# Attention, a gated MLP and a spatial-gating MLP on one core: small pooling and splitting work dealt out anew between VectorE, GpSimd and ScalarE, with a new order of the whole program

## The chip, the cores and the metric

The kernel runs on one core of one Trainium2 chip. The metric is the device time of one execution, in microseconds (us); smaller is better. The core has TensorE (PE: matmuls, and PEld its weight loads), VectorE (DVE), ScalarE (ACT), GpSimd (POOL) and SyncE (SP, which here issues all the transfers between DRAM and the on-chip memory). Each engine works through its own instructions in the order of its program and waits where a semaphore says that an operand, or a buffer, isn't ready.

## The reference

Eight batches of 576 positions, three parts that feed each other, all in float32:

```python
# 1. attention, 8 heads of 64, keys and values averaged over groups of 8 positions (72 of them)
k_p = k.reshape(B, H, 72, 8, D).mean(axis=3);  v_p = ... the same
attn = softmax(scale * q @ k_p^T);  x = attn @ v_p          # x: (8, 576, 512)
# 2. MLP with a convolution of width 3 along the positions as its gate
h = relu(x @ w_in)                                          # 512 -> 1024
x = (h * sigmoid(conv3(h))) @ w_out                         # 1024 -> 512
# 3. MLP with a spatial gate
h = gelu_tanh(x @ w_in2);  u, v = h[..., :512], h[..., 512:]
v_n = (v - mean(v)) / sqrt(var(v) + 1e-6) * g_ln            # over the 512 features
v_s = einsum('ts,bsd->btd', w_sg, v_n) + b_sg               # over the 576 positions
out = x + (u * v_s) @ w_out2                                # 512 -> 512
```

## The kernel before

Every float32 factor of a product is split into a high part, rounded to the matmul's input type, and a low part, the rest. A product is then three matmuls (high x high, low x high, high x low) summed in PSUM. So each operand costs a cast (mostly ACT) and a subtraction (`subtract`, L133, the instruction on L134; by DVE unless another engine is given).

The work goes in three stages that run into each other. Stage A (0 to about 540 us) is attention and the first MLP, batch after batch. `t_k` loads the keys of a batch in three blocks (`i` 0, 1, 2) and pools them with `pool_sum`: DVE does it in one reduction (L249), POOL as a tree of three additions (L251, L253, L255). For batch 0, DVE takes blocks 0 and 2 and POOL block 1. `t_kfin` transposes the pooled keys on PE (L292) and copies them to `KBT` with ACT (L295, L296) and DVE (L298, L301). The scores (L419), exponentials, their split (`eTh`, `eTl`), the attention product (L106 into `psa`), and the two matmuls of the MLP follow; their weights are loaded and split by `weight` along the way. Stage B (about 540 to 735 us) is the first matmul of the second MLP by a seven-product scheme. `t_v2` makes the v half of a block of rows: gelu on ACT, mean and variance on DVE (L804, L805), reciprocal deviation `rstd` on POOL (L808, L809), normalisation on DVE (L812), store to DRAM (`vs`, L816). It runs 18 times. Stage C (about 731 us to the end) loads the normalised v back (`vf`), forms sums on POOL (L948), splits them (`sc`: cast on ACT L617, subtraction L134), multiplies with the split `w_sg` (L767), lets DVE evict each quadrant with bias and gain (L997, into `tmp`) and POOL multiply it with u (L1001), splits the result (`g`) and does the last matmul (L99 to L101), to which DVE adds the residual (L1053). The 64 positions that don't fill a tile of 128 go through `t_vr` (`vr`: cast L956, subtraction of 64x512). `t_w_out2` loads and splits the four blocks of the last weight (`w4`, `w6`, `T3`, `T4`).

What sets the order is one long string, `ORDER`. Each part of the program (`t_k`, `t_v2`, ...) is a generator; a token such as `k1.0` or `n2.5` runs it to its next `yield`, and each engine's instructions are chained in the order in which the tokens issue them. Nothing reorders them later: an instruction that waits holds up whatever stands behind it on its engine. SP's transfers are chained likewise.

Of the kernel before, what the change touches and what calls it, by code (L numbers as in the profile page):

```python
# [11 lines left out]
AF = mybir.ActivationFunctionType  # L12
ALU = mybir.AluOpType
# [13 lines left out]
def pooled_attention_gated_mlps(  # L27
# [218 lines left out]
    def pool_sum(eng, raw, dst, n):  # L246
        a = raw[0:n]
        if eng is nc.vector:
            eng.tensor_reduce(out=dst, in_=a.rearrange("p a (r d) -> p a d r", r=POOL), axis=AX.X, op=ALU.add)  # L249
            return  # L250
        eng.tensor_tensor(out=a[:, :, 0:256], in0=a[:, :, 0:256], in1=a[:, :, 256:512], op=ALU.add)  # L251
        yield
        eng.tensor_tensor(out=a[:, :, 0:128], in0=a[:, :, 0:128], in1=a[:, :, 128:256], op=ALU.add)  # L253
        yield
        eng.tensor_tensor(out=dst, in0=a[:, :, 0:64], in1=a[:, :, 64:128], op=ALU.add)  # L255
# [3 lines left out]
    def t_k(i, b):  # L259

        n = (2, 2, 1)[i]
        P = 128 if i < 2 else 64
        if b > 1:
            raw = att2.tile([128, 2, 512], F32, tag="raw", name="raw")
        else:
            raw = staged(f"st{b}", n, ((in1, "xh", XW * KC), (slot, "hg", 2 * NF * CH))[b] if i == 0 else None)
        rows_ = k[b].rearrange("h (j r) d -> (h j) (r d)", r=POOL)[256 * i:256 * i + P * n]
        nc.sync.dma_start(out=raw[0:P, 0:n], in_=rows_.rearrange("(a p) x -> p a x", p=P))
        if b == 1:
            kv["k1", i] = raw  # L270
        yield
        if b == 1:
            return
        if ("kp", b) not in kv:
            kv["kp", b] = att1.tile([128, 5, D], F32, tag="kp", name="kp")
        eng = dve if b == 0 and i != 1 else pool
        yield from pool_sum(eng, raw[:, 0:n], kv["kp", b][0:P, 2 * i:2 * i + n, :], P)
# [495 lines left out]
    def t_v2(a, k):  # L773

        T = slice(128 * a, 128 * a + 128)
        n = 5 * k + min(2 * a + 1, 4)

        def mm(ps, m, first):
            x, w = xc[k, m], wc[1, m]
            passes(ps, [z for kt in range(2) for z in  # L780
                        three(x[:, 0, kt, T], x[:, 1, kt, T], w[:, 0, kt, :], w[:, 1, kt, :])], first, m in ENDS)

        tmp = tmps(n, FH)
        vg = outp.tile([128, 2, HF], F32, tag="ob", name="vg")
        keep = {}

        def ev(what, ps):
            if what in ("m1", "u2", "u3"):
                keep[what] = tmp(("m1", "u2", "u3").index(what))
                nc.scalar.copy(out=keep[what], in_=ps)  # L790
            elif what == "c21":
                nc.scalar.activation(out=vg[:, 0, FH:HF], in_=ps, func=AF.Gelu_apprx_tanh)
            else:
                o, u = {"c11": (vg[:, 0, 0:FH], "m1"), "c22": (vg[:, 1, FH:HF], "u3"), "c12": (vg[:, 1, 0:FH], "u2")}[what]
                nc.vector.tensor_tensor(out=o, in0=ps, in1=keep[u], op=ALU.add)

        yield from products(n, FH, mm, ev)
        nc.scalar.activation(out=vg[:, 0, 0:FH], in_=vg[:, 0, 0:FH], func=AF.Gelu_apprx_tanh)
        nc.scalar.activation(out=vg[:, 1, :], in_=vg[:, 1, :], func=AF.Gelu_apprx_tanh)
        yield  # L800
        st = stat.tile([128, 2, 6], F32, tag="st", name="st")
        mv = stat.tile([128, 2, 2], F32, tag="mv", name="mv")
        for j in range(2):
            nc.vector.bn_stats(out=st[:, j, :], in_=vg[:, j, :])  # L804
            nc.vector.bn_aggr(out=mv[:, j, :], in_=st[:, j, :])  # L805
        yield
        rs = stat.tile([128, 2], F32, tag="rstd", name="rstd")
        nc.gpsimd.tensor_scalar(out=rs, in0=mv[:, :, 1], scalar1=1e-6, scalar2=None, op0=ALU.add)  # L808
        nc.gpsimd.tensor_tensor(out=rs, in0=rs, in1=mhalf, op=ALU.pow)  # L809
        yield  # L810
        for j in range(2):
            nc.vector.tensor_scalar(out=vg[:, j, :], in0=vg[:, j, :], scalar1=mv[:, j, 0:1], scalar2=rs[:, j:j + 1],  # L812
                                    op0=ALU.subtract, op1=ALU.mult)
        yield
        r0 = XH * k + 128 * a
        nc.sync.dma_start(out=vs[r0:r0 + CH + 128, :].rearrange("(h p) d -> p h d", p=128)[:, 0:CT + 1:CT], in_=vg)  # L816
# [105 lines left out]
    def t_w_out2(i, *_):  # L922
        p, tag = ((slot, "w4"), (slot, "w6"), (w2["q"], "T3"), (w2["q"], "T4"))[i]
        return weight(p, tag, w_out2[128 * i:128 * i + 128, :], dve, i_bank, lambda hl: wo2.__setitem__(i, hl))
# [28 lines left out]
    def t_vr(_, b):  # L953
        x = vf[b, 0][:, 2]
        r = vrs[b] = w2["p"].tile([128, HF], F32R, tag=f"b{1 + b % 2}", name="vr")
        nc.scalar.copy(out=r, in_=x)  # L956
        yield
        subtract(r[REM:128], x[REM:128], r[REM:128])
# [161 lines left out]
```

## Time and profile before

| | us |
|---|---|
| median of three runs | 953.7 (951.04, 953.70, 954.91) |
| profiled execution, its own time | 952.67 |
| span of its trace | 950.9 |
| PE busy in the span | 918.5 (97%) |
| DVE, POOL, ACT busy | 759.8, 553.5, 527.6 |
| mean granted clock of PE | 0.993 |

The span is what lies between the first and the last recorded instruction; the execution's own time has 1.8 us more around it. PE is busy in all but 32.4 us of the span (950.9 less 918.5), so those 32.4 us and the clock of PE are all that an order alone can change.

### The profile page before, as it was taken

What the parts mean: (1) busy time and instruction counts of PE and PEld (TensorE: products, weight loads), DVE (VectorE), ACT (ScalarE), POOL (GpSimd) and SP (SyncE); (2) the same over time, 40 slices, a digit from 0 to 9 for tenths busy, and PEclk for the clock granted to TensorE, in tenths of its full rate; (3) what the DMA queues carried; (4) which work ended last, traced back from release to release, by engine and by line L of the source; (5) the groups of instructions that cost most, each with busy time, mean ns of one, the idle gap of its engine ahead of it and who ended that gap; (6) DMA issues with size and microseconds to landing.
All of it is one profiled execution on the core that took longest, in us unless ns stands there. A gap on an engine that the chain in (4) does not pass through costs nothing.

```text
span 950.9 us, 15815 instructions
## 1 busy us (share of the span) xinstructions
PE 918.5 (97%) x5396; PEld 838.4 (88%) x5396; DVE 759.8 (80%) x1399; ACT 527.6 (55%) x1108; POOL 553.5 (58%) x630
## 2 busy tenths in 40 slices
PE   5899999999999999999999999999999899999998
PEld 4787789988899899998998899999999898999886
DVE  5889988879879687787687878888787977878574
ACT  3666576766667576666655757655656432323211
POOL 3696788785868676557245375643553665555331
PEclk9899999999999999999999999999999999999999
DMA  9986293744635644424380475466537755565734
GB/s 230 251 197 149 62 186 114 178 133 139 153 119 139 142 119 100 129 59 117 99 170 34 94 144 141 151 184 200 146 111 230 246 176 190 158 192 173 231 115 142
DMA packets 185900, 143.61 MB, mean 151 GB/s; under 512 B 106048, under 2 KB 140124, under 8 KB 185820
## 3 DMA queue, kind: packets, MB, share of 16 engines
q1 hardware_dynamic: 185820, 142.61, 56.4%
q8 instruction: 42, 0.69, 0.3%
q14 instruction: 38, 0.31, 0.1%
HBM read 94.20 MB, written 48.37 MB: 150 GB/s over the span
## 4 chain that ended last, share of the span: by engine, by line
PE 77%; DVE 9%; DMA 6%; POOL 2%; ACT 2%; issue 2%; SPq 1%; DVEq 0%; POOLq 0%; ACTq 0%
PE psi L106 19%; PE pso L767 12%; PE psa L767 12%; PE pso L99 6%; PE pso L101 6%; PE pso L100 6%; PE psi L101 3%; PE psi L99 3%; PE psi L100 3%; PE psa L106 3%; PE psa L419 3%; DMA st<-in_v_dram 2%; DMA res<-x2s 1%; DMA wi1raw<-in_moe_w_in_dram 1%; DVE psi L571 1%
## 5 line engine op out<-in xcount | busy, mean ns | idle before, releaser
L134 POOL TENSOR_TENSOR hg<-g,hg 128x384 fp32r<-128x384 f32 x96 | 97.5, 1023 | 64.0 <-ACT hg L580 60.3
L1001 POOL TENSOR_TENSOR u<-u,tmp 128x288 f32<-128x288 f32 x64 | 61.8, 986 | 56.0 <-DVE tmp L997 39.8
L573 ACT ACTIVATE psi<-psi 128x384 f32<-128x384 f32 x96 | 46.1, 480 | 68.2 <-DVE psi L571 68.1
L570 DVE SCALAR_TENSOR_TENSOR psi<-h,coef,psi 128x384 f32<-128x384 f32 x96 | 58.9, 614 | 26.4 <-ACT psi L568 25.4
L134 POOL TENSOR_TENSOR eTl<-xb,eTh 128x512 fp32r<-128x512 f32 (+1 forms) x30 | 45.3, 1510 | 50.2 <-ACT eTh L503 50.1
L708 POOL TENSOR_TENSOR xb<-xb 128x768 f32<-128x768 f32 x24 | 45.9, 1912 | 48.2 <-DVE xc L134 30.2
L558 ACT ACTIVATE h<-psi 128x386 f32<-128x386 f32 (+1 forms) x96 | 47.3, 493 | 43.6 <-PE psi L106 43.3
L577 DVE SCALAR_TENSOR_TENSOR g<-psi,h 128x384 f32<-128x384 f32 x96 | 52.4, 546 | 20.0 <-ACT psi L573 18.1
L617 ACT CAST sc<-vf 128x512 fp32r<-128x512 f32 x48 | 28.8, 618 | 63.1 <-POOL vf L948 27.8
L571 DVE SCALAR_TENSOR_TENSOR psi<-h,coef,psi 128x384 f32<-128x384 f32 x96 | 59.8, 623 | 3.4
L419 PE MATMUL psa<-KBT,qT 128*128 128x144 f32 (+1 forms) x320 | 54.0, 299 | 5.2 <-ACT qT L401 1.8
L568 ACT ACTIVATE psi<-h,coef 128x384 f32<-128x384 f32 x96 | 56.2, 586 | 3.1
L419 PEld LDWEIGHTS psa<-KBT,qT 128*128 128x128 f32 (+1 forms) x320 | 45.2, 184 | 12.8 <-ACT qT L401 2.4
L580 ACT CAST hg<-g 128x384 fp32r<-128x384 f32 x96 | 47.7, 507 | 10.1 <-DVE g L577 10.0
L767 PE MATMUL pso<-wc,xc 128*128 128x256 f32 x378 | 51.1, 283 | 1.3 <-ACT tmp L790 0.9
L767 PE MATMUL psa<-wc,xc 128*128 128x256 f32 x378 | 50.7, 282 | 0.8 <-ACT tmp L790 0.5
L767 PEld LDWEIGHTS pso<-wc,xc 128*128 128x128 f32 x378 | 48.5, 189 | 2.5 <-ACT tmp L790 1.3
L1016 ACT CAST g<-u 128x256 fp32r<-128x256 f32 x64 | 22.3, 402 | 50.4 <-POOL u L1001 43.2
L767 PEld LDWEIGHTS psa<-wc,xc 128*128 128x128 f32 x378 | 48.6, 189 | 1.4 <-ACT tmp L790 0.7
L767 PE MATMUL psa<-xc,wc 128*128 128x384 f32 x252 | 48.2, 338 | 0.3 <-ACT tmp L834 0.3
L767 PE MATMUL pso<-xc,wc 128*128 128x384 f32 x252 | 48.3, 338 | 0.0
L457 POOL TENSOR_TENSOR en<-e,rs 128x512 f32<-128x512 f32 (+1 forms) x30 | 32.7, 1091 | 23.2 <-ACT h L558 8.5
(397 smaller groups left out, 3106.0 us busy)
## 6 DMA issues: line engine op xcount, KB each, us to landing
xb<-eds SPq DMA_DIRECT2D x24, 384.0 KB, 3.1
x2s<-ob SPq DMA_DIRECT2D x36, 256.0 KB, 2.8
us<-ub SPq DMA_DIRECT2D x24, 384.0 KB, 3.3
vs<-vg SPq DMA_DIRECT2D x18, 512.0 KB, 3.7
u<-us SPq DMA_DIRECT2D x16, 576.0 KB, 5.0
vf<-vs SPq DMA_DIRECT2D x16, 512.0 KB, 3.8
out_dram<-ob SPq DMA_DIRECT2D x32, 256.0 KB, 2.9
xb<-x2s SPq DMA_DIRECT2D x40, 192.0 KB, 4.3
```

Source lines behind the costliest of these rows:

```text
L99: nc.tensor.matmul(out=out_, lhsT=ah, rhs=bh, start=first, stop=False)
L100: nc.tensor.matmul(out=out_, lhsT=al, rhs=bh, start=False, stop=False)
L101: nc.tensor.matmul(out=out_, lhsT=ah, rhs=bl, start=False, stop=last)
L106: nc.tensor.matmul(out=out_, lhsT=a, rhs=b_, start=(i == 0), stop=(i == n - 1))
L134: eng.tensor_tensor(out=out, in0=in0, in1=hi.bitcast(F32), op=ALU.subtract)
L419: nc.tensor.matmul(out=ps[0:n, 2 * SP * x:2 * SP * x + 2 * SP], lhsT=qT[:, p, 0:n], rhs=KBT[:, p, :], start=True, stop=True)
L568: nc.scalar.activation(out=y, in_=tap(1), func=AF.Copy, scale=cw(1, f))
L570: nc.vector.scalar_tensor_tensor(out=y, in0=tap(0), scalar=cw(0, f), in1=y, op0=ALU.mult, op1=ALU.add)
L571: nc.vector.scalar_tensor_tensor(out=y, in0=tap(2), scalar=cw(2, f), in1=y, op0=ALU.mult, op1=ALU.add)
L577: nc.vector.scalar_tensor_tensor(out=go, in0=y, scalar=1.0, in1=tap(1), op0=ALU.add, op1=ALU.mult)
L767: nc.tensor.matmul(out=ps, lhsT=a, rhs=b_, start=first and i == 0, stop=last and i == n - 1, skip_group_check=True)
L1001: pool.tensor_tensor(out=z, in0=z, in1=o, op=ALU.mult)
```

## The change

Five things are changed. In `t_k`, block 1 of batch 0 is pooled by halves: its second 128 rows by DVE, its first 128 by POOL. In `t_v2`, for the last block of rows (two of the 18 calls), the normalisation is an activation of ACT, `rstd * v + (-mean * rstd)`, and POOL forms `-mean * rstd` in two more small operations; the other 16 calls compute as before. In `t_w_out2` the low parts of the four weight blocks go from DVE to POOL, and in `t_vr` the low parts of batches 0 and 1. And `ORDER` is another one throughout, in which every `n` task has one token more, for its additional `yield`.

```diff
@@ t_k
         eng = dve if b == 0 and i != 1 else pool
+        if b == 0 and i == 1:
+            yield from pool_sum(dve, raw[:, 1:2], kv["kp", b][:, 3:4, :], P)
+            n = 1
         yield from pool_sum(eng, raw[:, 0:n], kv["kp", b][0:P, 2 * i:2 * i + n, :], P)
@@ t_v2
         yield
-        for j in range(2):
-            nc.vector.tensor_scalar(out=vg[:, j, :], in0=vg[:, j, :], scalar1=mv[:, j, 0:1], scalar2=rs[:, j:j + 1],
-                                    op0=ALU.subtract, op1=ALU.mult)
+        if k == NBLK - 1 and a:
+            pool.tensor_tensor(out=mv[:, :, 0], in0=mv[:, :, 0], in1=rs, op=ALU.mult)
+            pool.tensor_scalar(out=mv[:, :, 0], in0=mv[:, :, 0], scalar1=-1.0, scalar2=None, op0=ALU.mult)
+            yield
+            for j in range(2):
+                nc.scalar.activation(out=vg[:, j, :], in_=vg[:, j, :], func=AF.Identity, scale=rs[:, j:j + 1],
+                                     bias=mv[:, j, 0:1])
+        else:
+            yield
+            for j in range(2):
+                nc.vector.tensor_scalar(out=vg[:, j, :], in0=vg[:, j, :], scalar1=mv[:, j, 0:1],
+                                        scalar2=rs[:, j:j + 1], op0=ALU.subtract, op1=ALU.mult)
@@ t_w_out2
-        return weight(p, tag, w_out2[128 * i:128 * i + 128, :], dve, i_bank, lambda hl: wo2.__setitem__(i, hl))
+        return weight(p, tag, w_out2[128 * i:128 * i + 128, :], pool, i_bank, lambda hl: wo2.__setitem__(i, hl))
@@ t_vr
-        subtract(r[REM:128], x[REM:128], r[REM:128])
+        subtract(r[REM:128], x[REM:128], r[REM:128], pool if b < 2 else dve)
@@ ORDER (one string, rewritten; a piece of its first line)
-... z z k0.1 p0.0 k1.0 p0.1 k1.0 k0.0 p0.0 k1.0 k2.1 k2.0 K.0 K.0 p1.0 ...
+... z z k0.1 v2.1 k1.0 k1.0 p0.0 k0.1 k1.0 k2.0 k0.0 K.0 p0.0 K.0 p1.0 ...
```

Lines of the kernel after stand 3 lower from `t_k` on, and 12 lower from the end of `t_v2` on (L298 becomes L301, L997 becomes L1009).

The first place is DVE at the start of the program, where it pools the keys of batch 0 (`st_138` holds the three blocks, `kp` the pooled keys) before it copies them to `KBT`; with each row stands the semaphore it waits for (DMAHW0, 1 and 2 are the transfers of blocks 0, 1 and 2). Before:

```order
L166 TENSOR_REDUCE small<-ident 96x4 [waits Pool_49]
L249 TENSOR_REDUCE kp<-st_138 128x128 [waits DMAHW0_49]
L249 TENSOR_REDUCE kp<-st_138 64x64 [waits DMAHW2_49]
L298 COPY KBT<-psa 64x3x72 [waits PE_49,Activation_49,Pool_49]
L301 COPY KBT<-psa 64x64 [waits PE_49]
```

And after:

```order
L166 TENSOR_REDUCE small<-ident 96x4 [waits Pool_49]
L249 TENSOR_REDUCE kp<-st_138 128x64 [waits DMAHW1_49]
L249 TENSOR_REDUCE kp<-st_138 64x64 [waits DMAHW2_49]
L249 TENSOR_REDUCE kp<-st_138 128x128 [waits DMAHW0_49]
L301 COPY KBT<-psa 64x3x72 [waits PE_49,Activation_49,Pool_49]
```

The reduction of block 0 (128x128) has moved from the first place to the last, behind the half of block 1 and block 2.

The second place is ACT about 205 to 211 us, where the pooled keys of a batch are copied to `KBT` among the relu (`h`), gate (`psi`) and cast (`hg`) of the first MLP. Before:

```order
L580 CAST hg<-g 128x384
L503 CAST eTh<-xb 128x6x4x32
L558 ACTIVATE h<-psi 128x386
L568 ACTIVATE psi<-h,coef 128x384
L295 COPY KBT<-psa 64x4x72
L296 COPY KBT<-psa 64x8
L558 ACTIVATE h<-psi 128x386
```

After:

```order
L506 CAST eTh<-xb 128x6x4x32
L298 COPY KBT<-psa 64x4x72
L299 COPY KBT<-psa 64x8
L583 CAST hg<-g 128x384
L561 ACTIVATE h<-psi 128x386
L571 ACTIVATE psi<-h,coef 128x384
```

The two copies have moved ahead of a relu and a gate instruction and stand right behind the cast of `eTh`.

The third place is DVE at the start of stage C, about 738 to 746 us, with the evictions (`tmp`) of the first two batches' products; `vg` are the last two normalisations of stage B. Before:

```order
L812 TENSOR_SCALAR vg_8375<-vg_8375,mv_8484,rstd_8519 128x512 x2
L997 SCALAR_TENSOR_TENSOR tmp0_8601<-pso_8581,coef_121,bsg_8323 128x288
L812 TENSOR_SCALAR vg_8414<-vg_8414,mv_8574,rstd_8618 128x512 x2
L997 SCALAR_TENSOR_TENSOR tmp1_8626<-psa_8489,coef_121,bsg_8323 128x288
L997 SCALAR_TENSOR_TENSOR tmp1_8636<-pso_8581,coef_121,bsg_8323 128x288
L134 TENSOR_TENSOR sc_8599<-vf_8595,sc_8599 128x512
L997 SCALAR_TENSOR_TENSOR tmp0_8549<-psa_8560,coef_121,tmp0_8549 128x288
L997 SCALAR_TENSOR_TENSOR tmp2_8659<-psa_8489,coef_121,bsg_8323 128x288
L134 TENSOR_TENSOR vr_8647<-vf_8595,vr_8647 64x512
L997 SCALAR_TENSOR_TENSOR tmp0_8601<-pso_8609,coef_121,tmp0_8601 128x288
```

After:

```order
L1009 SCALAR_TENSOR_TENSOR tmp1_8601<-psa_8484,coef_121,bsg_8388 128x288
L1009 SCALAR_TENSOR_TENSOR tmp0_8610<-pso_8567,coef_121,bsg_8388 128x288
L134 TENSOR_TENSOR sc_8591<-vf_8534,sc_8591 128x512
L1009 SCALAR_TENSOR_TENSOR tmp0_8555<-psa_8578,coef_121,tmp0_8555 128x288
L1009 SCALAR_TENSOR_TENSOR tmp1_8651<-pso_8567,coef_121,bsg_8388 128x288
L1009 SCALAR_TENSOR_TENSOR tmp2_8662<-psa_8484,coef_121,bsg_8388 128x288
L1009 SCALAR_TENSOR_TENSOR tmp0_8610<-pso_8623,coef_121,tmp0_8610 128x288
```

The two pairs of normalisations and the subtraction of `vr` are gone from between the evictions; the evictions themselves stand in nearly the order of before.

## Rows read from the trace of the kernel before

**Rows 1.** The page, busy time of each engine (us, share of the span, instructions):

```profile
PE 918.5 (97%) x5396; PEld 838.4 (88%) x5396; DVE 759.8 (80%) x1399; ACT 527.6 (55%) x1108; POOL 553.5 (58%) x630
```

**Rows 2.** Waits of PE by what ended them: us, times, longest us:

```profile
PE psa L397 <- DMA q<-in_q_dram: 8.5, 1, 8.5
...
PE psi L106 <- DVE g L577: 1.9, 4, 0.6
PE psa L419 <- ACT qT L401: 1.8, 2, 1.5
PE psa L106 <- DVE eTh L134: 1.2, 1, 1.2
```

**Rows 3.** Windows: us, busy us (instructions) PE, PEld, DVE, ACT, POOL; clock, DMA:

```profile
30.00:38.00 8.00, 6.95 (x28) 5.25 (x28) 5.79 (x12) 4.90 (x11) 6.68 (x13) 0.57 1.10 250
...
735.00:760.00 25.00, 22.33 (x161) 21.14 (x160) 23.39 (x45) 9.71 (x22) 15.02 (x14) 1.00 0.74 237
760.00:880.00 120.00, 120.00 (x715) 108.88 (x714) 95.18 (x178) 36.61 (x88) 67.53 (x60) 1.00 0.57 176
```

**Rows 4.** Timeline of DVE, start: start us, us, engine, instruction [idle before, releaser]:

```profile
4.52 1.87 DVE L249 TENSOR_REDUCE kp<-st 128x128 f32<-128x1024 f32 x1 [2.91 <-DMA st<-in_k_dram]
7.30 1.02 DVE L249 TENSOR_REDUCE kp<-st 64x64 f32<-64x512 f32 x1 [0.91 <-DMA st<-in_k_dram]
```

**Rows 5.** Timeline of POOL, start:

```profile
6.59 1.26 POOL L251 TENSOR_TENSOR st<-st 128x512 f32<-128x512 f32 x1 [3.81 <-DMA st<-in_k_dram]
...
8.73 0.45 POOL L255 TENSOR_TENSOR kp<-st 128x128 f32<-128x128 f32 x1
```

**Rows 6.** Timeline of PE, start:

```profile
9.38 1.30 PE L292 MATMUL psa<-ident,kp 128*64 128x128 f32 x5
```

**Rows 7.** Timeline of ACT about 30 us:

```profile
29.78 0.59 ACT L482 CAST eTh<-psa 128x512 fp32r<-128x512 f32 x1
```

**Rows 8.** Timeline of ACT about 208 us:

```profile
208.14 0.49 ACT L558 ACTIVATE h<-psi 128x386 f32<-128x386 f32 x1 [1.34 <-PE psi L106]
...
209.19 0.39 ACT L295 COPY KBT<-psa 64x288 f32<-64x288 f32 x1
```

**Rows 9.** Timeline of DVE about 210 us:

```profile
209.78 0.38 DVE L298 COPY KBT<-psa 64x216 f32<-64x216 f32 x1 [3.54 <-ACT KBT L296]
...
210.32 1.48 DVE L134 TENSOR_TENSOR eTh<-xb,eTh 32x256 fp32r<-32x256 f32 x1
```

**Rows 10.** Timeline of DVE about 220 us:

```profile
219.65 4.13 DVE L134 TENSOR_TENSOR eTh<-xb,eTh 32x256 fp32r<-32x256 f32 x1
```

**Rows 11.** Timeline of POOL about 220 us:

```profile
220.09 1.97 POOL L134 TENSOR_TENSOR hg<-g,hg 128x384 fp32r<-128x384 f32 x2
```

**Rows 12.** Timeline of DVE, start of stage C:

```profile
738.64 0.97 DVE L812 TENSOR_SCALAR vg<-vg,mv,rstd 128x512 f32<-128x512 f32 x2
...
745.11 0.81 DVE L134 TENSOR_TENSOR vr<-vf,vr 64x512 fp32r<-64x512 f32 x1
...
758.14 0.69 DVE L134 TENSOR_TENSOR T4hl<-t,T4hl 128x512 fp32r<-128x512 f32 x1
```

**Rows 13.** Timeline of PE, start of stage C, two of four waits:

```profile
750.53 1.06 PE L767 MATMUL pso<-sgc,sc 128*128 128x288 f32 x6 [1.11 <-DVE tmp L997]
759.50 1.06 PE L767 MATMUL pso<-sgp,sc 128*128 128x288 f32 x6 [0.77 <-DVE tmp L997]
```

**Rows 14.** POOL's groups by line and form, one of 16 like it (us, mean ns):

```profile
L134 POOL TENSOR_TENSOR w4hl<-t,w4hl 128x512 fp32r<-128x512 f32 x1 | 1.3, 1295 | 0.7 <-ACT w4hl L209 0.7
```

**Rows 15.** Timeline of POOL, start of stage C:

```profile
739.31 0.86 POOL L809 TENSOR_TENSOR rstd<-rstd,small 128x2 f32<-128x2 f32 x1
...
762.25 1.19 POOL L1001 TENSOR_TENSOR u<-u,tmp 128x288 f32<-128x288 f32 x1 [5.97 <-DVE tmp L997]
```

**Rows 16.** Timeline of ACT, start of stage C:

```profile
737.15 0.63 ACT L799 ACTIVATE vg<-vg 128x512 f32<-128x512 f32 x1 [0.78 <-DVE vg L795]
742.34 0.62 ACT L617 CAST sc<-vf 128x512 fp32r<-128x512 f32 x1 [4.56 <-DMA vf<-vs]
```

## What was predicted, before the changed kernel had run

> **What bounds the kernel now.** I read the busy times first. PE works 918.5 us of a span of 950.9 [rows 1], so only 32.4 us are idle, and no other engine comes near it over the whole. Then the waits of PE, to see where these 32.4 us lie [rows 2]. The largest, 8.5 us, is the wait for the first queries; nothing ahead of it is changed, so it stays. No other wait is over 1.5 us. Then windows of the stretches where the change does something [rows 3]. From 760 to 880 us PE is busy 120.00 of 120.00 us: it takes no notice of the small engines there, and whatever is won or lost before 760 us arrives at the end undiminished. From 735 to 760 us PE is busy 22.33 of 25 us, and DVE 23.39 of 25: here DVE is the bound, and PE loses 2.67 us to it. From 30 to 38 us the granted clock is 0.57, a mean of stretches at 2.4 and 1.2 GHz; PE was busy 6.95 us there, so at the full clock that work would take 0.57 x 6.95, and the dip costs at most 3.0 us. A change of small work can thus win a few us in all: it can fill waits of PE, and it can't shorten PE's work.
>
> **The start.** DVE now pools three pieces in the order half of block 1, block 2, block 0, though block 0 lands first: DVE began on it at 4.52 us, and POOL on block 1 at 6.59 when that had landed [rows 4, 5]. The half is a reduction of 512 numbers per partition like block 2's, so 1.02 us; block 0's is 1.87 [rows 4]. From 6.59 the three in a row end at 6.59 + 1.02 + 1.02 + 1.87 = 10.50 us. Before, the last pooled keys were POOL's, at 8.73 + 0.45 = 9.18 [rows 5], hidden behind the transposes of the queries, and PE went on to transpose the keys at 9.38 [rows 6]. PE's order is the same there, so the keys' transposes, the copies and the first scores come 10.50 - 9.38 = 1.1 us later. POOL's tree over half the rows is done before DVE and sets nothing. Part of this comes back. At 30.7 us PE waits 1.5 us for a copy of `qT` on ACT [rows 2], which stood behind the cast of `eTh`, 0.59 us [rows 7]; now the copy is ahead of the cast. I count 0.5 of the 0.59, the rest overlapping. Net +0.6 us. The bounds are +1.5 (nothing comes back, and the next copy, which now stands behind a weight's cast, is later too) and -3.0 (the clock's dip goes). I don't take the dip as gone, since PE idles as long at the start as before.
>
> **The keys at 209 us.** PE waits 1.24 us (1.2 in the list) for `eTh` [rows 2]. Behind that stands DVE, idle 3.54 us until ACT's copies to `KBT` [rows 9]; and ACT made them at 209.19 because a relu stood ahead that waited 1.34 us for PE [rows 8]. Now the copies stand ahead of relu and gate. ACT was idle from 206.8, so they can come 2.4 us sooner, more than the 1.24. I take -1.1 us; bounds -1.2 and 0 (DVE's `eTh` takes 1.48 us there, and may be stretched again).
>
> **Two engines, one memory port.** At 219.65 us a subtraction of 32x256 on DVE took 4.13 us [rows 10]; the same form took 1.48 at 210 [rows 9]. Beside the long one POOL ran subtractions back to back [rows 11]. The rows don't tell the cause, but DVE operations with two operands in the on-chip memory are long where POOL is busy. The change gives POOL more of such work. At this place itself POOL's train stands in after's order much as before, so 0, with bounds -1.5 and +1.5.
>
> The Trainium skill has a rule for this. Its page "SBUF — State Buffer", section "Who interferes with whom", says that VectorE and GpSimd share one pair of ports under an exclusive lock, and that a VectorE operation with two inputs there blocks against a GpSimd operation that reads there. "Perfetto Trace Analysis", section "Optimizing Scalar/DVE Operations", concludes that moving work between the two might not help. The 4.13 us agree with it. By that rule stage C below would win nothing.
>
> **The start of stage C, 735 to 760 us.** Off DVE go two pairs of normalisations, about 0.97 each [rows 12]; two subtractions of `vr`, 0.81 for the one shown, the other like it; and those of `T4` and `T3`, 0.69 each [rows 12]. That is 2 x 0.97 + 2 x 0.81 + 2 x 0.69 = 4.9 us. Not all of it stood in PE's way: the normalisations end before 741.5, and at 743 DVE waited for ACT anyway, so they are worth nothing here by themselves. In the way stood the `vr` ahead of the evictions that PE waits for up to 750.53 us, 1.11 us there, and `T4` ahead of the eviction behind the 0.77 us at 759.50 [rows 13]. The removed 0.81 and the 0.77 make 1.6 us; the two small waits before 750 lose part as well, as DVE's subtractions run at 0.81 rather than 0.69 beside POOL. I take -2.0; bounds -2.7 (all of PE's idle time) and 0 (the lock).
>
> What is added: on POOL, a low part of 128x512 costs 1.3 us [rows 14], sixteen of which the trace shows; `vr` of 64x512 has as many elements per partition, so 1.3. Two `vr`, `T4` and `T3` make 5.2 us in a stretch where POOL was busy 15.02 of 25 us [rows 3], with 5.97 idle just before 762.25 [rows 15]: `T4` and `T3` go there at no cost, and the second `vr` puts off u's multiplications by 1.3 us, whose results are wanted only by the matmuls of about 760. `w4` and `w6`, earlier, go beside a saturated PE: nothing. The four small operations of POOL for `-mean * rstd` take at most 0.86 each like `rstd`'s [rows 15]. On ACT the normalisation is four activations of 128x512 at 0.63 [rows 16], 2.5 us; ACT was idle 4.56 us before 742.34, and the first pair fits in. The second pair stands behind six casts of `sc` and `vr`, so the last stores of v go out about 750 and the loads queued behind them on SP a little later; these load for the third batch, and POOL's first multiplication for it was at 762.25 [rows 15]. If that cover is gone, each us of lateness is a us. I take 0, bounds 0 and +2.
>
> **The rest of the order.** Four waits for `g`, 1.9 us [rows 2], come where DVE is nearly always busy; in one, a weight's bit operation that stood ahead of `g` now follows it, in the others something else does. I take 0, bounds -1.5 and +1.5.
>
> **The sum.** 952.67 + 0.6 - 1.1 + 0 - 2.0 + 0 + 0 = 950.2 us, against the profiled execution's own 952.67 (span 950.9 and 1.8 around it). The median of the three runs is 953.7, 1.0 us higher. So 950.2, and a us more is as well possible: 3.5 us or 0.4% under the median. A measurement of this kernel can't tell less than 0.5%, 4.8 us, from no change: the borders are 948.9 and 958.5.
>
> **Rivals.**
> 1. The dip of the clock goes as well. The start is rearranged where the dip is (PE's work at 30 to 38 us, V of batch 1 loaded sooner), and for it speaks that PE's wait of 1.5 us just at 30.7 gets shorter; against it, that PE starts 1.1 us later after the same idle time. With -3.0 and another -0.7 from stage C: 946.5.
> 2. The moved subtractions are worth nothing, because DVE then waits as long for the port as it had worked. For it, the 4.13 us and the 0.81 instead of 0.69; against it, that a normalisation moved to ACT, not POOL, and the evictions read PSUM. Without the 2.0: 952.2. The Trainium skill's rule in "SBUF — State Buffer", above, comes to the same.
> 3. Slower: trains of POOL's operations block DVE where DVE is the bound. The price of one collision is 4.13 - 0.7 (an undisturbed subtraction, taken as `T4`'s) = 3.4 us of DVE. At 735 to 760 POOL's four new operations, 5.2 us, against 3.0 of work removed in their place (2 x 0.81 + 2 x 0.69), cost 2.2 instead of winning 2.0; with one collision of 3.4 elsewhere in stage A that PE has to wait for: 952.67 + 0.6 - 1.1 + 2.2 + 3.4 = 957.8. It decides from the point where POOL's subtraction starts ahead of an eviction's predecessor while PE has no spare bank. Against it, PE paid under 2 us for the 4.13.
> 4. The change does something else than it says: the order is different everywhere, and in stage A PE's small waits are replaced by others of the same size with the start's 1.1 us on top and 209's gain lost elsewhere. 954 us.
>
> **How the numbers follow.** My forecast 0.45 (its own range 948 to 952), rival 1 0.23, rival 2 0.13, rival 3 0.11, rival 4 0.08. Faster than 948.9 are nearly all of rival 1 (0.21) and a third of the forecast's (0.14): 0.35. Slower than 958.5 are two fifths of rival 3, and mishaps that I don't see, 0.10 in all. Same has the rest, 0.55. For 8 in 10 the range goes from 945, past rival 1, to 957, short of the worst of rival 3.
>
> **What would show it.** Start: DVE's 128x128 reduction ends at about 10.5 us and the keys' transposes follow. 209: no wait of PE for `eTh`, and DVE's idle 3.5 us gone. Stage C: PE's waits for `tmp` from 735 to 760 sum to under 1 us, and from there PE runs without a gap. Wrong would be: DVE subtractions over 2 us in stages where PE waits for them; ACT's normalisation waiting with casts of `sc` late behind it; a second dip of the clock; or a new wait of over 2 us for a transfer.

## The result, and the profile after

The changed kernel takes 943.97 us, median of four runs (942.78 to 944.80), against 954.24 for the kernel before on the same chip (four runs, 951.04 to 954.91): a ratio of 0.9898, interval 0.9873 to 0.9923. Measured once more on another chip, beside the experiments, it was 944.94 against 952.26: 0.9926 (0.9909 to 0.9942). So the change wins 7 to 10 us; the second figure rests on 20 runs of the kernel before and is the surer. 3.5 were forecast, and the time lies 1 us outside the range of 945 to 957.

The profiled execution of after took 944.80 us, its span 943.0. Busy times, to be read beside [rows 1], and the granted clock in 40 slices:

```profile
PE 912.6 (97%) x5396; PEld 834.9 (89%) x5396; DVE 751.7 (80%) x1390; ACT 532.3 (56%) x1112; POOL 563.4 (60%) x640
...
PEclk9999999999999999999999999999999999999999
```

PE has the same 5396 matmuls and is idle for 943.0 - 912.6 = 30.4 us, only 2.0 less than before. It is busy 5.9 us less: its mean granted clock is 0.999, against 0.993 before, with no dip that the windows show.

To see where the time went, I followed seven matmuls, each with the same matmuls ahead of it in both kernels. Columns: start us, duration, engine, line, instruction, idle time before it and its releaser. Before:

```profile
114.58 0.45 PE L106 MATMUL psi<-xh,wi1hl 128*128 128x388 f32 x1 [0.42 <-DVE g L577]
...
170.95 0.34 PE L106 MATMUL psi<-xh,wi5hl 128*128 128x386 f32 x1
...
255.05 0.45 PE L106 MATMUL psi<-xh,wi5hl 128*128 128x388 f32 x1
...
550.71 0.39 PE L99 MATMUL pso<-w7hl,hg 128*128 128x512 f32 x1
...
729.02 0.85 PE L767 MATMUL psa<-wc,xc 128*128 128x256 f32 x5 [0.46 <-ACT tmp L790]
...
763.79 0.39 PE L99 MATMUL psi<-T4hl,g 128*128 128x512 f32 x1
...
945.84 0.40 PE L101 MATMUL psi<-T4hl,gr 128*128 128x512 f32 x1
```

And after:

```profile
113.30 0.44 PE L106 MATMUL psi<-xh,wi1hl 128*128 128x388 f32 x1 [0.76 <-DVE g L580]
...
171.49 0.34 PE L106 MATMUL psi<-xh,wi5hl 128*128 128x386 f32 x1
...
250.04 0.44 PE L106 MATMUL psi<-xh,wi5hl 128*128 128x388 f32 x1
...
546.73 0.39 PE L99 MATMUL pso<-w7hl,hg 128*128 128x512 f32 x1
...
723.35 0.86 PE L770 MATMUL psa<-wc,xc 128*128 128x256 f32 x5 [0.46 <-ACT tmp L793]
...
757.36 0.39 PE L99 MATMUL psi<-T4hl,g 128*128 128x512 f32 x1
...
937.99 0.40 PE L101 MATMUL psi<-T4hl,gr 128*128 128x512 f32 x1
```

The differences are -1.3, +0.5, -5.0, -4.0, -5.7, -6.4 and -7.9 us. So after wins 1.3 us up to 114, loses 1.8 up to 171, wins 5.5 up to 255, loses 1.0 up to 551, wins 1.7 up to 729 (stage B), 0.8 up to 764 (the start of stage C) and 1.4 behind that. The largest piece lies at 171 to 255 us, where the prediction had 1.1.

**171 to 255 us.** Windows of before (columns as in [rows 3]):

```profile
190.00:255.00 65.00, 62.10 (x325) 54.60 (x323) 55.53 (x98) 41.85 (x83) 48.66 (x64) 0.97 0.50 131
231.00:236.00 5.00, 4.96 (x19) 4.43 (x20) 4.83 (x11) 3.67 (x12) 2.17 (x3) 0.66 0.71 204
```

Windows of after, there, at two places of [rows 3], and at 130 us:

```profile
30.00:38.00 8.00, 5.38 (x36) 3.53 (x34) 6.45 (x14) 6.16 (x17) 6.50 (x11) 1.00 1.00 232
130.00:150.00 20.00, 18.34 (x94) 15.56 (x93) 17.66 (x29) 12.61 (x25) 16.56 (x19) 1.00 0.59 172
190.00:255.00 65.00, 65.00 (x348) 58.24 (x349) 54.90 (x106) 45.18 (x88) 53.57 (x68) 1.00 0.57 146
735.00:760.00 25.00, 22.20 (x154) 21.08 (x153) 22.15 (x42) 11.33 (x24) 18.06 (x17) 1.00 0.77 230
```

In these 65 us PE of before was idle 2.90 us, and its clock fell to 1.2 GHz from 231.8 to 235.2 us, which cost half of 3.4, some 1.7 us. After has neither. 1.24 of the 2.90 are the wait for `eTh` at 209 [rows 2]. The rest are four small waits, which in before came 3 to 7 us behind the long subtraction of [rows 10] and just ahead of the dip:

```profile
226.59 0.45 PE L106 MATMUL psi<-xh,wi0hl 128*128 128x388 f32 x1 [0.27 <-DVE g L577]
...
228.86 0.45 PE L106 MATMUL psi<-xl,wi0hl 128*128 128x388 f32 x1 [0.23 <-DVE xl L533]
229.91 0.40 PE L106 MATMUL psa<-eTh,Vh 128*128 128x288 f32 x1 [0.43 <-ACT eTh L503]
...
231.04 0.40 PE L106 MATMUL psa<-eTl,Vh 128*128 128x288 f32 x1 [0.73 <-POOL eTl L134]
```

The idle time and the dip make 4.6 of the 5.5 us; the rest is not accounted for.

In after that subtraction takes 0.61 us. But another of its kind, at 131 us, is now held, that is, takes several times its own length beside POOL. DVE of after (the copy to `KBT` and the `eTh` behind it answer to [rows 9], the last row to [rows 10]):

```profile
131.39 3.88 DVE L134 TENSOR_TENSOR eTh<-xb,eTh 32x256 fp32r<-32x256 f32 x1
...
207.18 0.38 DVE L301 COPY KBT<-psa 64x216 f32<-64x216 f32 x1 [0.43 <-ACT KBT L299]
...
207.71 1.13 DVE L134 TENSOR_TENSOR eTh<-xb,eTh 32x256 fp32r<-32x256 f32 x1
...
218.65 0.61 DVE L134 TENSOR_TENSOR eTh<-xb,eTh 32x256 fp32r<-32x256 f32 x1
```

POOL of after beside the one at 131 us:

```profile
130.55 1.05 POOL L460 TENSOR_TENSOR en<-e,rs 128x512 f32<-128x512 f32 x1
131.56 0.30 POOL L464 TENSOR_TENSOR en<-e,rs 128x64 f32<-128x64 f32 x1
131.81 1.55 POOL L134 TENSOR_TENSOR eTl<-xb,eTh 128x512 fp32r<-128x512 f32 x1
...
133.78 1.00 POOL L134 TENSOR_TENSOR hg<-g,hg 128x384 fp32r<-128x384 f32 x1
134.86 1.54 POOL L134 TENSOR_TENSOR VR<-vrm,VR 32x512 fp32r<-32x512 f32 x1
...
218.67 0.91 POOL L253 TENSOR_TENSOR raw<-raw 64x128 f32<-64x128 f32 x1
```

Each operation of POOL starts before the one ahead is recorded as ended, until the last: 133.78 + 1.00 = 134.78, and the next starts at 134.86. DVE's subtraction ends at 135.27, 0.49 us behind 134.78, the end ahead of that first gap. This train, and the waits of PE behind it (18.34 of 20 us busy at 130 to 150, where before has 19.89), are where after loses its 1.8 us. At 218.65 it is POOL that is held: its addition takes 0.91 us beside DVE's 0.61. In before the same addition, at the same place, took half of that, and DVE 4.13:

```profile
219.67 0.45 POOL L253 TENSOR_TENSOR raw<-raw 64x128 f32<-64x128 f32 x1
```

**The start.** DVE's three reductions end at 6.66 + 3.74 = 10.40 us, and PE's transposes of the keys come at 10.45, against [rows 6]:

```profile
6.66 3.74 DVE L249 TENSOR_REDUCE kp<-st 128x64 f32<-128x512 f32 x3 [5.05 <-DMA st<-in_k_dram]
```

```profile
10.45 1.31 PE L295 MATMUL psa<-ident,kp 128*64 128x128 f32 x5 [0.97 <-DVE kp L249]
```

**The start of stage C.** PE of after, to be read beside [rows 13], two waits in all:

```profile
739.17 1.06 PE L770 MATMUL pso<-sgp,sc 128*128 128x288 f32 x6 [1.35 <-DVE tmp L1009]
...
743.00 1.06 PE L770 MATMUL psa<-sgc,sc 128*128 128x288 f32 x6 [1.45 <-DVE tmp L1009]
```

They sum to 2.80 us, no less than the 2.67 of before, and only 0.8 us are won from 729 to 764 us. The 1.7 us ahead of that lie in stage B, where PE of before waits six times, 2.27 us in all, and PE of after three times, 1.30 us. One of before's waits, 0.33 us at 644.25, follows the low part of `w6`, for which DVE took 2.32 us at 640.62 (`T4`'s took 0.69 [rows 12]); `e2`, below, where POOL makes it, has no such wait.

### The profile page after: what moved, and what is told of

It is laid out like the page before. It is cut to its first block, busy times and chain, and to the rows that moved or that the text cites. A ratio compares the mean times of both kernels' runs of the same rounds, so it can differ in the third digit from the quotient of the medians.

```text
span 943.0 us, 15842 instructions
## 1 busy us (share of the span) xinstructions
PE 912.6 (97%) x5396; PEld 834.9 (89%) x5396; DVE 751.7 (80%) x1390; ACT 532.3 (56%) x1112; POOL 563.4 (60%) x640
## 4 chain that ended last, share of the span: by engine, by line
PE 84%; DMA 5%; DVE 5%; POOL 2%; ACT 1%; issue 1%; SPq 1%; DVEq 0%; POOLq 0%; ACTq 0%
PE psi L106 21%; PE pso L770 12%; PE psa L770 12%; PE pso L99 7%; PE pso L101 7%; PE pso L100 7%; PE psa L106 5%; PE psi L99 4%; PE psi L101 4%; PE psi L100 3%; PE psa L422 3%; DMA q<-in_q_dram 1%; DMA qb<-in_q_dram 1%; DMA st<-in_v_dram 1%; DMA vf<-vs 1%
## 5 line engine op out<-in xcount | busy, mean ns | idle before, releaser
L134 POOL TENSOR_TENSOR hg<-g,hg 128x384 fp32r<-128x384 f32 x96 | 100.5, 1057 | 66.8 <-ACT hg L583 64.6
L1013 POOL TENSOR_TENSOR u<-u,tmp 128x288 f32<-128x288 f32 x64 | 59.5, 950 | 48.6 <-DVE tmp L1009 42.1
L506 ACT CAST eTh<-xb 128x768 fp32r<-128x768 f32 (+1 forms) x30 | 41.1, 1370 | 14.6 <-DVE xb L502 14.5
```

The costliest lines, as they stand in the source:

```text
L134: eng.tensor_tensor(out=out, in0=in0, in1=hi.bitcast(F32), op=ALU.subtract)
L1013: pool.tensor_tensor(out=z, in0=z, in1=o, op=ALU.mult)
```

## The experiments

The kernels were timed beside the kernel before, on three chips: the first four runs on one, `e5` to `e12` on another, `e13` to `e15` on a third. Since the kernel before itself takes 951.4 to 952.6 there, the ratios compare best.

| run | what it is | median us (lowest to highest, runs) | ratio to before, interval |
|---|---|---|---|
| e1 | after's order, engines of before | 949.71 (948.63–950.26, 12) | 0.9977 (0.9966–0.9988) |
| e2 | before's order, four moves of engine | 953.81 (950.50–955.50, 12) | 1.0014 (1.0000–1.0029) |
| e3 | before, 183 to 241 us from after | 948.92 (946.98–951.27, 12) | 0.9976 (0.9964–0.9988) |
| e4 | after, 183 to 241 us from before | 949.27 (948.14–950.58, 12) | 0.9975 (0.9964–0.9985) |
| e5 | after again | 944.94 (944.30–945.08, 6) | 0.9926 (0.9909–0.9942) |
| e6 | before, one subtraction moved to POOL | 951.17 (947.67–953.05, 12) | 0.9987 (0.9973–1.0000) |
| e7 | after, one subtraction moved to POOL | 942.57 (942.08–943.14, 5) | 0.9902 (0.9884–0.9921) |
| e8 | after, normalisations and `vr` on DVE | 948.25 (946.81–948.61, 9) | 0.9949 (0.9929–0.9969) |
| e9 | before, the first 55 us from after | 950.08 (948.59–951.07, 12) | 0.9971 (0.9960–0.9982) |
| e10 | after, the first 55 us from before | 945.60 (944.35–949.36, 6) | 0.9938 (0.9918–0.9958) |
| e11 | after, low parts of the last weights on DVE | 946.47 (945.71–947.32, 6) | 0.9941 (0.9927–0.9955) |
| e12 | e7, and key block 0 pooled first | 940.79 (940.73–941.19, 4) | 0.9882 (0.9866–0.9899) |
| e13 | before, two subtractions moved to POOL | 947.41 (945.64–948.98, 12) | 0.9954 (0.9938–0.9969) |
| e14 | after, normalisations alone on DVE | 946.44 (946.17–947.27, 7) | 0.9945 (0.9924–0.9965) |
| e15 | e13, the first 55 us from after | 945.88 (944.22–946.53, 6) | 0.9936 (0.9912–0.9959) |

### e1 and e2: the order alone, the moves alone

`e1` keeps after's `ORDER` and undoes the moves; `e2` keeps before's `ORDER` and makes them (less the added `yield`).

```diff
...
-        if k == NBLK - 1 and a:
+        if False:
...
-        return weight(p, tag, w_out2[128 * i:128 * i + 128, :], pool, i_bank, ...)
+        return weight(p, tag, w_out2[128 * i:128 * i + 128, :], dve, i_bank, ...)
...
-        subtract(r[REM:128], x[REM:128], r[REM:128], pool if b < 2 else dve)
+        subtract(r[REM:128], x[REM:128], r[REM:128])
```

> The new order with every operation on the engine it had before (block 1 of the keys pooled by GpSimd alone, all normalisations and the low parts of w4, w6, T3, T4 and vr on VectorE). Theory 'order': the gain of 10 us comes from the new order, so nearly all of it stays: 943 to 947 us. Theory 'engines': the operations taken off VectorE carry at least half of it: 949 us or more.

> The order of before with the four changes of engine (the two small GpSimd operations stand with the reciprocal deviation, the ScalarE normalisation where VectorE's stood). Theory 'order': within 3 us of the kernel before, 952 to 957 us. Theory 'engines': 949 us or less.

The order alone wins 2 us of the 7 to 10, the moves alone nothing: `e1` lies where 'engines' put it, `e2` where 'order' did, and neither theory holds by itself. `e1` keeps up with after to about 610 us and then falls behind. PE of `e1` at the start of stage C:

```profile
736.99 1.85 PE L767 MATMUL pso<-sgc,sc 128*128 128x288 f32 x12 [0.42 <-DVE tmp L1006]
...
744.16 1.06 PE L767 MATMUL psa<-sgc,sc 128*128 128x288 f32 x6 [1.47 <-DVE tmp L1006]
...
748.50 1.06 PE L767 MATMUL pso<-sgc,sc 128*128 128x288 f32 x6 [1.95 <-DVE tmp L1006]
```

The new order puts DVE's second pair of normalisations among the evictions, and there it costs PE 3.84 us of waits against after's 2.80. In `e2` it is the other way about: DVE has less to do and stands idle, waiting for PE itself, at the same place:

```profile
739.37 0.52 DVE L1008 SCALAR_TENSOR_TENSOR tmp<-pso,coef,bsg 128x288 f32<-128x288 f32 x1 [1.42 <-PE pso L770]
...
741.05 0.52 DVE L1008 SCALAR_TENSOR_TENSOR tmp<-pso,coef,bsg 128x288 f32<-128x288 f32 x1 [0.73 <-PE pso L770]
```

PE's waits for `tmp` sum to 2.58 us in `e2` (before: 2.67). So at this place the moves pay only with the order that was written for them.

### e3 and e4: the stretch of 183 to 241 us alone

The tokens of `ORDER` for one stretch (from 794 to about 1032 of before's) are put in the other order. As the two orders have not issued the same work at its ends, tokens are left out or added there, so that everything is issued once; the edits reach to token 1066 in `e3` and 1213 in `e4`. The engines stay as in the kernel named.

```diff
-ORDER = '''... (before's tokens 794 to 1032) ...
+ORDER = '''... (after's tokens for the same work) ...
```

> The kernel before, engines and order, except that the tokens of the stretch from about 183 to 241 us stand in the new order. Theory 'order', sharpened: that one stretch holds 6 of the 10 us, since PE has no wait and no dip of the clock in it after: 948 us (946.5 to 950), granted clock 1.0 from 190 to 237 us, and no subtraction of eTh over 2 us there. Theory 'engines', and a third one that the gain is spread evenly over the program: 953 us or more.

> The kernel after with the stretch from about 183 to 241 us in the order of before. Theory 'order', sharpened: it loses 6 us, 950 us (948 to 952), with PE's wait for eTh at about 211 us and the dip of the clock after 230 us back. Theories 'engines' and 'spread evenly': 944 to 946 us.

`e4` loses 4 to 5 us of after's gain: PE's wait for `eTh` is back (1.24 us at 212.23), the subtraction at 220 us is held again, for 4.02 us, and the clock dips from 231.4 to 234.8. In its profile `e3` wins over 4 us on before between 171 and 235 us and gives most of it back by 255. Its median lies in the expected range, but two other subtractions are held, just outside the window that the expectation named: one for 3.87 us at 185.56 and the one shown here. DVE and, below, PE of `e3`:

```profile
239.66 4.00 DVE L134 TENSOR_TENSOR eTh<-xb,eTh 32x256 fp32r<-32x256 f32 x1
```

```profile
246.21 0.44 PE L106 MATMUL psi<-xh,wi4hl 128*128 128x388 f32 x1 [2.02 <-DVE g L577]
```

The wait ends 2.5 us behind the hold's end, and the clock dips behind it, from 246.8 to 250.2 us: the same sequence as in before at 220 to 235, at another place. The stretch nets only some 0.5 us in this pair of profiles, so that most of `e3`'s 2.6 us by the medians is not shown to come from it.

### e5: after again

No edit; it measures after on the chip of the runs that follow.

> The kernel after once more, as the measure for the others on this chip, since the kernel before stood at 951.5 us in the last comparison and at 954.2 where the change was timed. If the gain is a property of the kernels: 941 to 944 us, ratio 0.989 to 0.991. If part of it belongs to the chip: 945 us or more.

At 0.9926 it misses the 0.989 to 0.991 of the first theory: some of the 10 us of the first comparison belonged to that comparison, of four runs of each kernel. Its profile has a dip of the clock at 30 to 36 us (mean 0.72), as before's had, and its own time is 944.30; the first profile of after has no dip there and 944.80, on another chip. Behind the dip the two run together: the matmul shown at 113.30 starts at 113.16 in `e5`, and at 113.64 in `e11`, which has the dip from 30.4 to 37.2 us. So in after's order the early dip costs 0.3 to 0.5 us at most.

### e6, e7 and e13: the held subtraction on POOL

```diff
-        subtract(eh[R, NP_:NP_ + 2], m[R, NP_:NP_ + 2], eh[R, NP_:NP_ + 2])
+        subtract(eh[R, NP_:NP_ + 2], m[R, NP_:NP_ + 2], eh[R, NP_:NP_ + 2],
+                 pool if (t, b) == (3, 3) else dve)
```

That is `e6`: the subtraction at 220 us of before. `e7` has `(0, 2)`, the one at 131 us, in after; `e13` has `in ((3, 3), (0, 4))`, in before.

> The kernel before with a single subtraction (eTh 32x256 of the fourth tile of batch 3, 4.13 us at 219.65 us) given to GpSimd, same order. Theory 'block': VectorE is held there by GpSimd's train; PE's waits from 226 to 231 us (1.7 us) and the dip of the clock behind them (3.4 us at half speed, 1.7 us) follow from it, so the kernel gets 3 us faster: 947 to 949.5 us. Rival 'order': these waits come from the places of other instructions; no change, 950.5 to 953 us.

> The kernel after with a single subtraction (eTh 32x256 of the first tile of batch 2, 3.88 us at 131.39 us) given to GpSimd. Theory 'block': the new order has moved the block to 131 us, where it costs the waits at 136.0 and 140.8 us (1.6 us) and some more; 1.6 to 2.7 us faster than e5_after. Rival: no change against e5_after (within 0.8 us).

> The kernel before with two subtractions on GpSimd: the one of e6_before_one_sub (at 219.65 us) and the first tile of batch 4, which was held 3.68 us at 245 us in that run. Theory 'block returns': e6 won only 1.1 us because the hold came back there and cost PE 1.7 us; without it the kernel is 4 to 5 us below the kernel before (0.9945 to 0.996). Rival: a hold is worth about 1 us; 0.9975 to 0.9990.

In `e6` the waits at 226 to 231 us and the dip behind them are gone, which wins 4.3 us in the profiles, but the next of these subtractions is held, and 2.0 us are given back by 255. (This profile also lost 3.4 us at its start, before the edit could matter, with a wait of 2.40 us that is shown below and the clock at 0.57 from 44 to 48 us.) DVE, then PE, of `e6`:

```profile
245.09 3.68 DVE L134 TENSOR_TENSOR eTh<-xb,eTh 32x256 fp32r<-32x256 f32 x1
```

```profile
251.32 0.45 PE L106 MATMUL psi<-xh,wi4hl 128*128 128x388 f32 x1 [1.70 <-DVE g L578]
```

`e13` moves that one as well. No hold over 1.71 us is left, and PE's busy time in the window at 190 to 255 us (before: 62.10 us at a clock of 0.97) is

```profile
190.00:255.00 65.00, 63.77 (x346) 57.23 (x345) 54.50 (x104) 44.63 (x87) 53.53 (x70) 1.00 0.56 148
```

with the 1.24 us for `eTh` at 209 left over. That is worth 4 us: 947.41 against 951.44. In `e7` the loss at 130 to 150 us is gone (after: 18.34 busy), and the time is 2.4 us under `e5`'s:

```profile
130.00:150.00 20.00, 19.97 (x106) 17.61 (x105) 15.89 (x30) 14.70 (x27) 18.36 (x23) 1.00 0.58 172
```

`e13` also shows a short hold, on DVE and POOL:

```profile
132.47 1.20 DVE L134 TENSOR_TENSOR eTh<-xb,eTh 32x256 fp32r<-32x256 f32 x1
```

```profile
132.44 0.75 POOL L253 TENSOR_TENSOR raw<-raw 128x256 f32<-128x256 f32 x1
133.26 1.54 POOL L134 TENSOR_TENSOR VR<-vrm,VR 32x512 fp32r<-32x512 f32 x1
```

POOL's gap comes at 133.19, and the same instruction that was held for 3.88 us in after ends at 133.67, again 0.48 us behind the end of POOL's operation ahead of the gap.

### e8, e14 and e11: which moves pay

`e8` takes the normalisations and the low parts of `vr` back to DVE, `e14` the normalisations alone, `e11` the low parts of the last weights. The lines are those of `e1`'s diff, one or two at a time, in after.

> The kernel after with the last normalisations and all low parts of vr on VectorE again, the four weight blocks still on GpSimd. From e1_order_only the moves of engine are worth 5 us within the new order. Theory 'start of stage C': normalisations and vr carry 3 us of it (PE's waits for tmp from 735 to 750 us grow from 2.8 to 5 us or more). Theory 'weights': w4, w6, T3 and T4 carry it, and this kernel is within 1 us of e5_after.

> The kernel after with the last two pairs of normalisations on VectorE, vr on GpSimd. e8_after_norm_vr_dve, both on VectorE, stood at 0.9949 against 0.9926 for the kernel after. If the normalisations carry it, since the new order puts the second pair between evictions that PE waits for: 0.9943 to 0.995. If vr does: 0.9925 to 0.9932.

> The kernel after with the low parts of w4, w6, T3 and T4 on VectorE again. Of the 5 us that the moves of engine are worth in the new order, e8_after_norm_vr_dve accounts for 3.3; if the rest is the weights', this kernel is 1.5 to 2 us slower than the kernel after (0.994 to 0.995 of the kernel before), with PE's waits between 610 and 660 us back. Rival: the pooling by halves carries the rest, and this one is within 0.7 us of the kernel after.

Against after's 0.9926, `e14` loses 0.0019 (1.8 us) and `e8` 0.0023 (2.2 us; 3.3 between the medians, which are from one chip): the normalisations carry it, and `vr` adds little. The intervals overlap, so the sizes are rough; the profiles agree with them. From after's matmul at 723.35 to the one at 757.36 `e14` takes 1.9 us more than after and `e8` 2.4. The rows show the way. DVE of `e14`, between the subtractions and evictions of stage C:

```profile
744.46 1.96 DVE L824 TENSOR_SCALAR vg<-vg,mv,rstd 128x512 f32<-128x512 f32 x2
```

The pair takes twice the 0.97 us of before [rows 12]. Behind it PE waits again at 746.90, for 1.19 us; after has no wait there. `e11` loses 1.4 us (interval again overlapping; 1.6 in the profiles from after's matmul at 546.73 to the one at 723.35), and PE shows waits in stage B that after does not have:

```profile
636.52 1.68 PE L770 MATMUL psa<-wc,xc 128*128 128x256 f32 x12 [0.32 <-DVE ub L856]
...
649.65 2.01 PE L770 MATMUL pso<-xc,wc 128*128 128x384 f32 x10 [0.39 <-DVE xc L134]
```

### e9, e10, e12 and e15: the start

`e9` and `e10` exchange the first 243 tokens of `ORDER`, with a few behind them so that everything is issued once; `e15` does `e9`'s edit in `e13`; `e12` is `e7` with one token moved:

```diff
-... i0 i1 z z k0.1 v2.1 k1.0 k1.0 p0.0 k0.1 k1.0 k2.0 k0.0 K.0 p0.0 ...
+... i0 i1 z z k0.1 v2.1 k0.0 k1.0 k1.0 p0.0 k0.1 k1.0 k2.0 K.0 p0.0 ...
```

> The kernel before, engines included, with the first tokens (to about 55 us) in the new order. The runs of the kernel before scatter over 5 to 8 us and those of the kernel after over 1 to 2, and the profiles of the old start differ in a wait of 0.4 to 2.4 us near 41 us, for a transfer or for the split of a weight behind it. Theory 'start': the new start takes this wait away; the runs lie within 2.5 us of each other and the median is 2 us or more below the kernel before. Rival: the scatter comes from later; scatter and median as before (within 1 us).

> The kernel after with the first tokens (to about 55 us) in the order of before. Theory 'start': 2 us or more slower than the kernel after (0.9926 of the kernel before in e5_after, so here 0.994 to 0.996) and the runs scatter over 4 us or more. Rival: as the kernel after, 0.991 to 0.9935, scatter under 2 us.

> The kernel before with the new order of the first 55 us and the two subtractions of e13_before_two_subs, no other change of engine. If start (2.5 us in e9_before_new_start) and holds (4 to 5 us) add up: 0.992 to 0.9935, as fast as the kernel after without any of its moves of engine. If they overlap: 0.9945 to 0.997.

> The kernel after with two things mended: the subtraction of e7_after_one_sub on GpSimd (which won 2.4 us), and at the start the key block that lands first pooled first. By the working of the prediction the keys' transposes then start about 9.4 us instead of 10.45, 1 us sooner: 3 to 3.5 us below the kernel after, 0.9885 to 0.9895 of the kernel before. Rival: the 1 us is swallowed by a later wait of the start, 0.990 (as e7_after_one_sub).

The new start wins 2.5 us in before (`e9`), and 1.5 by medians on top of `e13` (`e15`). Taken out of after (`e10`) it costs 0.7, with an interval that holds none as well as 2 us: the direction and the scatter (5.0 us) are those of the expectation, the size is not settled. What it removes stands about 41 us, where PE of before, and below it of `e6`, waits for the V of batch 1, or for a weight's split that stands behind V's work on DVE:

```profile
41.55 0.91 PE L106 MATMUL psa<-st,ident 128*128 128x128 f32 x6 [0.61 <-DMA st<-in_v_dram]
```

```profile
43.48 2.93 PE L106 MATMUL psa<-st,ident 128*128 128x128 f32 x15 [2.40 <-DVE pso L149]
```

The profiles with the old start show 0.4 to 2.4 us there, those with the new one none: SP now issues V of batch 1 from 24.8 us in one piece, where before the last of it began at 29.2. `e12` undoes the one thing that delays the keys, and PE's transposes of them come at 9.24 us instead of 10.45, with no wait for `kp`. It wins 1.8 us on `e7`, a little more than expected. At 0.9882 `e12` is the fastest version here, ahead of after on the same chip by 4.2 us. `e15` comes near after (0.9936 against 0.9926) without one of its moves of engine; it lies between the two ranges expected.

## Why the prediction was wrong

The sign was right, the size was not: -3.5 us against -7 to -10. By its own terms:

- **Two engines, one memory port, at 219.65 us: this step failed.** The prediction saw the 4.13 us, said that "POOL's train stands in after's order much as before, so 0", and bounded it by 1.5 either way. But the hold went. What holds the subtraction seems to be a matter of less than a tenth of a us: whether it or POOL's next addition comes first (the last section has the numbers), and no order of instructions shows that. And the price was not only the wait that could be seen behind it: 1.7 us of small waits, and 1.7 us of the dip at 231.8 to 235.2, which the prediction did not have, since it read the clock only at 30 to 38 us. `e13` puts the holds at 4 us in before, `e7` that at 131 us, for which the prediction had nothing either, at 2.4 in after. Part of the gain, then, is that the one hold costs less where it stands now. The prediction had named a DVE subtraction of over 2 us that PE waits for as a sign of being wrong.
- **The keys at 209 us: right.** The copies to `KBT` came 2.7 us sooner, DVE's idle time of 3.54 became 0.43, and PE's wait of 1.24 is gone, -1.1 forecast.
- **The start: one part right, the sum of the wrong sign.** Forecast +0.6. The keys came 1.1 us later, as said, and `e12` won 1.8 by undoing it. But the loads of V of batch 1, which the prediction named only for rival 1, took away a wait near 41 us: -1.3 in the pair of profiles, and by the medians -2.5 in `e9`, -1.5 in `e15` and -0.7 in `e10`. The profiles with the old start differ by almost 5 us among themselves at 114 us, so the medians are the better witness.
- **Stage C: too large.** Forecast -2.0, found -0.8 between 729 and 764 us. PE's waits for `tmp` did not fall under 1 us, as the prediction wanted; they are 2.80. The subtractions of `sc` beside POOL took up to 1.42 us. The normalisations, called "worth nothing here by themselves", carry 1.8 us (`e14`), because the new order would have put them where the evictions stand.
- **Stage B: a term put at nothing without a window of it.** Forecast 0, found -1.7 between 551 and 729 us. The four low parts of weights, beside "a saturated PE: nothing", are worth 1.4 within the new order (`e11`).
- **ACT's normalisation** takes 0.76 us (1.51 for two), not 0.63, and the added work cost nothing that can be seen, as forecast.
- **The rest of the order.** The waits for `g` went from 1.9 to 2.8 us, inside the bounds. Behind 764 us the pair of profiles differs by 1.4 us more, most of it a wait of before, 1.13 us at 899.84 for `sc`. That is not the change's: `e2`, `e3`, `e6` and `e13` have before's order there and no such wait, `e9` has 0.40 us. The prediction's reading of its window to 880 us stands.
- **Rival 1** gave nearly the right time for the wrong reason: the dip at 30 us did go in one profile, but `e5` is as fast with it. PE of after was busy only 5.38 of 8 us there, so other engines set the pace. **Rival 2** fails as a forecast of the time, 952.2. At the start of stage C it was nearer than the forecast, as PE's waits show; but the weights' low parts win on POOL (`e11`), and so does a held subtraction that the change had left on DVE, 2.4 us in `e7`. The rival is also the rule of the Trainium skill ("SBUF — State Buffer", "Who interferes with whom"). The long hold agrees with that rule in kind, since the subtraction has two operands in the on-chip memory and lasted as long as POOL's train. **Rival 3** named the mechanism that decided, but only as a loss: collisions can be taken away as well.

Put together, as an estimate: -4.0 (`e13`) and +2.4 (`e7`) for the two holds, -1.2 at 209, -1.3 at the start, -1.7 in stage B and -0.8 at the start of stage C make -6.6 us, against the 7.0 to 7.3 of the second comparison.

Left open: the lock was not tested by itself, with all else equal; the holds only agree with it. Nor is it settled which edit cost the 1.0 us between 255 and 551 us (a wait of 0.54 us at 458.91 is half of it), nor what makes the clock dip at 30 us in some executions.

## What to carry to other kernels

Look through a group for the single instruction that takes several times its fellows' time beside another engine's unbroken train, and price all that follows it, the later waits and the clock among them; a small shift of order can remove it or make it anew elsewhere, so judge it in the changed trace and move the victim rather than the order. Judge moves of engine together with the order they were made for: here the moves alone won nothing, the order alone 2 us, both 7 to 10. And look at a stage's own window before you call its edits free.

## What the runs showed of the hardware

- A DVE subtraction of 32x256, 0.6 us when free, took 3.7 to 4.1 us in fifteen places of these profiles, beside POOL operations that follow each other without a gap. In all fifteen it ended 0.47 to 0.49 us behind the end of POOL's last operation ahead of a gap (0.08 us in after, 4.7 in before). Holds of 1 to 2 us mostly ended otherwise, without a gap: at 331.26 us of after the subtraction took 1.96 us and ended beside an addition of POOL that took 0.80 us in place of 0.46. What lets DVE in between two operations of POOL in one place and not in another is not shown. DVE's evictions from PSUM keep their length beside the same POOL: the groups of `tmp` have a mean of 509 to 512 ns in both kernels, while subtractions of `sc` next to them take 0.81 to 1.42 us.
- Which engine is held seems to be decided within a tenth of a us. At the subtraction of [rows 10], ten profiles with after's order there (after, `e1`, `e3`, `e5`, `e7`, `e8`, `e10`, `e11`, `e12`, `e14`) have DVE starting 0.02 to 0.06 us ahead of POOL's addition; DVE takes 0.61 to 0.64 us, and the addition 0.87 to 0.93. Four with before's order (before, `e2`, `e4`, `e9`) have it from 0.02 ahead to 0.10 behind; DVE takes 4.02 to 4.13 us, and the addition 0.45 or 0.46. At 0.02 ahead both were seen, so that is as fine as the records tell. The two groups differ in the order around the place as well, and the starts were not varied by themselves.
- The dip of the clock in mid-program came behind the small waits of PE that follow a hold: at 231.8 us in before, 229.9 in `e9`, 230.6 in `e2`, 231.4 in `e4`, 246.8 in `e3`. In `e6`, `e7` and `e13`, where these waits are missing, there is none at 231. After's waits behind its own hold, 0.5 us at 136 and 1.1 at 140.75, were followed by no dip, nor was the 1.70 us of `e6` at 251; what makes the difference is not shown.
- The kernels with the old start scatter more: before ran from 949.07 to 957.51 us on one chip (20 runs), after from 944.30 to 945.08 (6). Over 12 runs each, `e2` with the old start spans 5.0 us, `e9` with the new one 2.5.
